# Attention's value products: the two heads of a pair in turn, key block by key block

## The chip, the cores and the metric

The kernel runs on one core of a Trainium2 chip. The time is device microseconds (us) of one execution on that core. Three runs of the kernel before took 1001.0, 1001.56 and 1004.53 us; the median is 1001.56.

## The reference, cut to what matters

```python
# q, k, v: [batch 4, heads 8, seq 576, head_dim 64]
scores = q @ k.transpose(0, 1, 3, 2) / sqrt(64)
rel = pos[:, None] - pos[None, :]
mask = (rel >= 0) & (rel < 128)                 # each query sees itself and 127 keys before it
scores = where(mask, scores - slopes[h] * abs(rel), -1e9)
attn = softmax(scores)
x = attn @ v                                    # -> [2304 tokens, 8 * 64 = 512]
x = (silu(x @ w_gate) * (x @ w_val)) @ w_out    # layer 1, hidden 1536
h = x @ w_in                                    # layer 2, hidden 2048
return (h * tanh(softplus(h))) @ w_out2
```

## The kernel before, in words

The 2304 tokens (four sequences of 576) are cut into five chunks of 512, 384, 512, 512 and 384 (`A_CHUNKS`). They are numbered 0 to 4 here. Three phases follow each other. The attention of chunk 0 runs alone (to about 59 us). Then layer 1 runs over the chunks (to about 637 us), and during layer 1 of chunk c the attention of chunk c+1 is mixed in. Layer 2 is last and has no attention in it.

Attention of a chunk works on query blocks of at most 128. For each head there are three kinds of work on TensorE, each as "pieces" that a planner places:

- S (`score`, lines 204 to 234): scores of one PSUM bank into `s_ps`. VectorE adds the bias and takes the row minimum (L226), ScalarE takes the exponential (L230); after the head's last bank come `norm` and the splitting of the next head's q and k.
- T (`transp`, L251): the normalised weights `Pt` are transposed by TensorE into `t_ps` (L259), and ScalarE copies them to `PT` (L271).
- O (`outp`, L274): the value products. The 64 value dimensions of head 0 of a pair go to partitions 0 to 63 of the bank `o_ps`, those of head 1 to partitions 64 to 127. Each key block contributes one product: its values `v` (up to 128 keys by 64) are the weights, and the columns of `PT` that belong to the queries seeing that block are streamed. ScalarE and VectorE then write the two halves of `xt` (a rounded part and the rest), and the values of the pair after next are loaded by DMA on SyncE's queue (`load_v`, L181).

The operands of O are plain fp32, and each product is executed as two passes, each with a weight load (LDWEIGHTS) and a MATMUL. There are four O pieces per chunk. For one head of one pair the key blocks (keys x streamed columns) are, in the order before:

- chunk 0: 128x256, 128x256, 128x256 and 128x128, in order of `par`;
- chunk 1: 64x64, 128x256, 64x64, 128x64, 128x192;
- chunk 2: 128 keys throughout, two of 256 columns and three of 128;
- chunk 3: 128x256, 64x64, 128x192, 128x128, 128x192, 64x64;
- chunk 4: 128 keys throughout, two of 256 columns and two of 128.

The sum of the columns over two heads and two passes is 3584, 2560, 3584, 3584 and 3072.

Layer 1 consists of groups of 12 products: two "g" groups (`g_ps`, `hid`) per hidden tile, and one "o" group (`acc`, `proj`). TensorE's instructions stand in the order in which the program emits them (`manual_schedule`, L912). The loop from L985 emits one group and then as many attention pieces as the planner's costs allow: pieces are spread so that the share of their cost that is spent keeps pace with the share of groups done (L998). S pieces have costs 1.7 or 0.87, T 0.44, and O the number of key blocks times 0.86 (`o_piece`, L356). The order on the other engines is worked out by a scheduler from this program. The banks of `g_ps`, `s_ps`, `t_ps` and `o_ps` rotate through four buffers (`rot`).

Of the kernel before, what the change touches and what calls it, by code (L numbers as in the profile page):

```python
# [37 lines left out]
def chunk_plan(t0, n):  # L38

    segs, qb, kb = [], [], []  # L40
    done = 0
    koff = 0
    while done < n:
        b, s0 = divmod(t0 + done, S)
        m = min(n - done, S - s0)
        kn0 = min(W, s0)
        segs.append(SimpleNamespace(b=b, s0=s0, n=m, c0=done, kn0=kn0, koff=koff))
        first = len(qb)
        prevkb = None
        if kn0:  # L50
            prevkb = SimpleNamespace(b=b, k0=s0 - kn0, n=kn0, uses=[], par=1, seg=len(segs) - 1)
            kb.append(prevkb)
        o = 0
        while o < m:
            qn = min(W, m - o)
            q0 = s0 + o
            kn = min(W, q0)
            q = SimpleNamespace(qn=qn, kn=kn, c=done + o, ko=koff + kn0 + o - kn, idx=len(qb))
            own = SimpleNamespace(b=b, k0=q0, n=qn, uses=[], par=(len(qb) - first) % 2, seg=len(segs) - 1)
            if prevkb is not None:  # L60
                prevkb.uses.append((q, 0))
            own.uses.append((q, 1))
            qb.append(q)
            kb.append(own)
            prevkb = own
            o += qn
        done += m
        koff += kn0 + m
    for i, x in enumerate(kb):
        x.vi = i  # L70
        x.w = sum(q.qn for q, _ in x.uses)
        assert all(q.kn == x.n for q, o in x.uses if o == 0)
        assert all(x.uses[i + 1][0].c == x.uses[i][0].c + x.uses[i][0].qn for i in range(len(x.uses) - 1))
    nbanks = -(-sum(q.kn + q.qn for q in qb) // 512)
    sb = [[[], 0] for _ in range(nbanks)]
    for q in sorted(qb, key=lambda q: -(q.kn + q.qn)):
        x = next(x for x in sb if x[1] + q.kn + q.qn <= 512)
        q.so = x[1]
        x[0].append(q)
        x[1] += q.kn + q.qn  # L80
    order = sorted(kb, key=lambda x: (x.n != 128))
    full = [x for x in order if x.n == 128]
    part = [x for x in order if x.n != 128]
    nbanks = -(-sum(x.w for x in kb) // 512)
    tb = [[[], 0] for _ in range(nbanks)]
    for x in sorted(full, key=lambda x: -x.w) + part:
        i = next(i for i in range(nbanks) if tb[i][1] + x.w <= 512)
        x.bank = i
        x.bo = tb[i][1]
        tb[i][0].append(x)  # L90
        tb[i][1] += x.w
    o_order = sorted(kb, key=lambda x: x.par)
    return SimpleNamespace(t0=t0, n=n, segs=segs, qb=qb, kb=kb, sb=sb, tb=tb, o_order=o_order, nk=koff)


# [1 line left out]
def body(ctx: ExitStack, tc: tile.TileContext, qT, kT, vP, w1, w1o, w2, cst, yT):  # L97
# [18 lines left out]
    def mm(out, lhsT, rhs, start, stop):  # L116
        nc.tensor.matmul(out=out, lhsT=lhsT, rhs=rhs, start=start, stop=stop, skip_group_check=True)  # L117

    def rot(name):
        return ps.tile([128, 512], F32, tag="rot", name=name)  # L120


    def hi_act(out, in_):
        return nc.scalar.activation(out=out, in_=in_, func=AF.Copy)  # L124

    def lo_dve(out, in_, hi):
        return nc.vector.tensor_tensor(out=out, in0=in_, in1=hi.bitcast(F32), op=ALU.subtract)  # L127
# [3 lines left out]
    for n in A_CHUNKS:  # L131
        plansA.append(chunk_plan(t, n))
        t += n
# [4 lines left out]
    def attention(ap, p, ci, s_native, upfront):  # L138


        raw, qk, pt_, P_, sums = {}, {}, {}, {}, {}
# [132 lines left out]
        def outp(pr):  # L274
            v = raw.pop(("v", pr))
            xt = x_t[ci]
            n = p.n
            o_ps = rot("o_ps")
            for e in range(2):
                st = True  # L280
                for x in p.o_order:
                    c0 = x.uses[0][0].c
                    mm(
                        o_ps[64 * e:64 * e + 64, c0:c0 + x.w], v[:x.n, x.vi, 64 * e:64 * e + 64],
                        pt_[2 * pr + e, x.bank][:x.n, x.bo:x.bo + x.w], st, False,
                    )
                    st = False
            hi_act(xt[:, 0, pr, :n], o_ps[:, :n])
            lo_dve(xt[:, 1, pr, :n], o_ps[:, :n], xt[:, 0, pr, :n])

        return SimpleNamespace(
            ci=ci, load=load, load_v=load_v, split=split, score=score, norm=norm, transp=transp,
            outp=outp, upfront=upfront, ns=len(p.sb), nt=len(p.tb), s_full=s_full, nk=len(p.kb),
        )

    early = {}

    def attention_pieces(atts):

        heads = [(a, h) for a in atts for h in range(H)]  # L300
        pairs = [(a, r) for a in atts for r in range(HP)]
        n = len(heads)
        out = []

        def run(k, f):
            a, h = heads[k]
            return getattr(a, f)(h)

        def load(k):
            if not heads[k][0].upfront:  # L310
                run(k, "load")

        def load_v(r):
            if not pairs[r][0].upfront:
                pairs[r][0].load_v(pairs[r][1])

        def first():
            if atts[0].upfront:
                for h in range(0, H, 2):
                    run(h, "load")  # L320
                    for f in early.pop(h, []):
                        f()
            load(0)
            load_v(0)
            run(0, "split")
            load(1)
            load_v(1)

        def s_piece(k, g):
            a, h = heads[k]  # L330

            def f():
                if k == 0 and g == 0:
                    first()
                a.score(h, g)
                if g == a.ns - 1:
                    a.norm(h)
                    if k + 1 < n:
                        run(k + 1, "split")
                        if k + 2 < n:  # L340
                            load(k + 2)

            return (a.ci, 1.7 if a.s_full(h) else 0.87, f)

        def o_piece(k):
            a, h = heads[k]

            def f():
                if a.ci not in x_t:
                    x_t[a.ci] = xp.tile([128, 2, CT, 512], F32R, tag="x", name="xt")  # L350
                a.outp(h // 2)
                r = a.ci * HP + h // 2 + 2
                if r < len(pairs):
                    load_v(r)

            return (a.ci, a.nk * 0.86, f)  # L356

        def t_piece(k, g):
            a, h = heads[k]
            return (a.ci, 0.44, lambda: a.transp(h, g))  # L360

        def delay(k):
            return CFG["delay0"] if heads[k][0].ci == 0 else 1

        for st in range(n + 4):
            todo = {"S": [], "T": [], "O": []}
            if st < n:
                todo["S"] = [s_piece(st, g) for g in range(heads[st][0].ns)]
            for k in range(max(0, st - 4), min(st, n)):
                if k + delay(k) == st:  # L370
                    todo["T"] += [t_piece(k, g) for g in range(heads[k][0].nt)]
                if k + delay(k) + 1 == st and heads[k][1] % 2 == 1:
                    todo["O"].append(o_piece(k))
            for c in CFG["order"]:
                if todo[c]:
                    out.append(todo[c].pop(0))
            for c in "SOT":
                out += todo[c]
        out.sort(key=lambda x: x[0] > 0)
        return out  # L380
# [531 lines left out]
    with tc.manual_schedule(engines={mybir.EngineType.PE}):  # L912
# [26 lines left out]
        while at < lasts[0]:  # L939
# [11 lines left out]
            f = (at / lasts[0] - CFG["conv_a"]) / (CFG["conv_b"] - CFG["conv_a"])  # L951
# [3 lines left out]
        for ci, p in enumerate(plansA):  # L955
# [29 lines left out]
            for gi, (kind, i, f) in enumerate(groups):  # L985
# [12 lines left out]
                while win and (spent * ng < (gi + 1) * total or gi == len(groups) - 1):  # L998
                    _, cost, e = win.popleft()
# [78 lines left out]
```

## Time and profile before

| what | value |
|---|---|
| runs | 1001.0, 1001.56, 1004.53 us |
| profiled execution, from first to last instruction (span) | 1002.2 us |
| TensorE (PE) busy | 966.8 us, 96% |
| VectorE (DVE) busy | 706.7 us, 71% |
| ScalarE (ACT) busy | 555.0 us, 55% |
| GpSimd (POOL) busy | 137.4 us, 14% |
| chain that ended last | PE 29% of the span, DVE 2%, DMA 1% |

The span is all that the profile tells of its execution's time. It lies 0.6 us above the median of the runs and inside their spread, so nothing outside the span has to be added. PE is the matmul side of TensorE and PEld its weight loads, which can overlap matmuls. A matmul's end is modelled in the profile: one that streams 256 columns is shown as some 0.38 us long while the next starts earlier. So times of matmuls are read here from start to start.

### The profile page before, as it was taken

The numbers are of one execution on the slowest core, as the hardware profiler recorded it, in microseconds if no ns is written. First come the engines' busy times: TensorE is split into PE (matmuls) and PEld (weight loads), VectorE is DVE, ScalarE is ACT, GpSimd is POOL, SyncE is SP. The second block draws the span as 40 slices with busy tenths as digits, with TensorE's granted clock in tenths as the row PEclk, the third lists the DMA queues.
The fourth block names the chain that finished last, engine by engine and source line by source line (L and its number), as shares of the span: only waits on it lengthen the run. The fifth ranks groups of instructions, "written<-read, shape, count | busy, mean of one in ns | idle before, by whom it ended". The sixth has DMA issues, their size and how long they took to land. (4 is left out here: it accounts for less than half of the span.)

```text
span 1002.2 us, 14578 instructions
## 1 busy us (share of the span) xinstructions
PE 966.8 (96%) x5168; PEld 854.4 (85%) x5168; DVE 706.7 (71%) x1263; ACT 555.0 (55%) x1135; POOL 137.4 (14%) x204
## 2 busy tenths in 40 slices
PE   6899999999999999999999999899999999999998
PEld 4557777898997877788787999789999999999998
DVE  4989898686586644647843576787795888867773
ACT  6857566666677555544643345555463555545342
POOL 2610000000000000000001233454002330022000
PEclk8989999999999999999999999999999999999999
DMA  8854433566454632326610898432787137850275
GB/s 303 283 208 146 136 120 114 183 214 199 129 166 152 215 110 69 101 65 227 233 43 22 298 374 293 169 116 84 243 260 254 64 109 269 291 172 22 82 248 195
DMA packets 76920, 174.82 MB, mean 174 GB/s; under 512 B 9136, under 2 KB 52528, under 8 KB 67120
## 3 DMA queue, kind: packets, MB, share of 16 engines
q1 hardware_dynamic: 76848, 173.90, 51.9%
q8 instruction: 40, 0.66, 0.3%
q14 instruction: 32, 0.26, 0.1%
HBM read 138.22 MB, written 35.65 MB: 173 GB/s over the span
## 5 line engine op out<-in xcount | busy, mean ns | idle before, releaser
L117 PE MATMUL g_ps<-xt,w 128*128 128x512 f32 (+1 forms) x1440 | 316.4, 372 | 1.1 <-ACT PT L271 1.1
L117 PEld LDWEIGHTS g_ps<-xt,w 128*128 128x128 f32 x1440 | 258.4, 188 | 38.0 <-ACT PT L271 2.2
L117 PE MATMUL bk<-xs,win 128*128 128x384 f32 x1008 | 179.1, 336 | 7.5 <-DVE G L679 5.4
L117 PEld LDWEIGHTS bk<-xs,win 128*128 128x128 f32 x1008 | 174.4, 188 | 11.8 <-DVE G L679 9.0
L117 PE MATMUL bk<-op,wout 128*128 128x384 f32 x1008 | 175.5, 334 | 0.5 <-DMA wout<-w2o 0.5
L117 PEld LDWEIGHTS bk<-op,wout 128*128 128x128 f32 x1008 | 174.8, 188 | 0.8 <-issue 0.8
L117 PE MATMUL acc<-hh,ring 128*128 128x512 f32 (+1 forms) x480 | 149.4, 374 | 1.6 <-DVE ring L127 1.6
L124 ACT ACTIVATE op<-G 128x768 fp32r<-128x768 f32 x84 | 70.8, 846 | 65.6 <-PE bk L117 63.1
L117 PEld LDWEIGHTS acc<-hh,ring 128*128 128x128 f32 x480 | 88.9, 188 | 15.4 <-DVE ring L127 2.3
L127 DVE TENSOR_TENSOR op<-G,op 128x768 fp32r<-128x768 f32 x84 | 80.5, 965 | 26.9 <-ACT op L124 26.3
L117 PE MATMUL acc<-hl,ring 128*128 128x512 f32 (+1 forms) x240 | 88.4, 368 | 0.0
L230 ACT ACTIVATE Pt<-Pt,sm 128x256 f32<-128x256 f32 (+2 forms) x160 | 74.3, 466 | 14.8 <-DVE sm L226 14.5
L613 ACT ACTIVATE t<-g_ps 128x512 f32<-128x512 f32 (+1 forms) x60 | 32.9, 549 | 78.8 <-PE g_ps L117 78.6
L614 DVE SCALAR_TENSOR_TENSOR t<-t,g_ps 128x512 f32<-128x512 f32 (+1 forms) x60 | 37.7, 629 | 53.0 <-ACT t L613 53.0
L226 DVE CUSTOM_DVE_ANT_0 Pt<-s_ps,cst_sb 128x256 f32<-128x256 f32 (+2 forms) x160 | 54.2, 376 | 27.7 <-PE s_ps L117 19.4
L775 POOL TENSOR_TENSOR t<-w 128x256 f32<-128x256 f32 x48 | 42.5, 905 | 224.1 <-DVE win L127 211.3
L622 DVE SCALAR_TENSOR_TENSOR t<-t,g_ps 128x512 f32<-128x512 f32 (+1 forms) x60 | 37.9, 632 | 37.0 <-PE g_ps L117 36.0
L1023 ACT ACTIVATE G<-G 128x384 f32<-128x384 f32 x72 | 36.8, 520 | 44.4 <-DVE G L679 44.4
L679 DVE TENSOR_TENSOR G<-u,bk 128x384 f32<-128x384 f32 x72 | 39.0, 552 | 31.3 <-PE bk L117 29.2
L124 ACT ACTIVATE hh<-t 128x512 fp32r<-128x512 f32 (+1 forms) x60 | 34.9, 582 | 43.8 <-DVE t L622 43.8
L259 PE MATMUL t_ps<-cst_sb,Pt 128*128 128x128 f32 (+2 forms) x288 | 47.0, 279 | 7.7 <-POOL Pt L249 4.2
L247 ACT ACTIVATE Pt<-Pt,sm 128x256 f32<-128x256 f32 (+2 forms) x128 | 50.1, 465 | 7.1 <-DVE sm L241 7.0
(75 smaller groups left out, 1250.8 us busy)
## 6 DMA issues: line engine op xcount, KB each, us to landing
wout<-w2o SPq DMA_DIRECT2D x42, 1024.0 KB, 6.4
wraw<-w SPq DMA_DIRECT2D x16, 1024.0 KB, 5.7
w2o<-chl SPq DMA_DIRECT2D x16, 896.0 KB, 8.7
wst<-w SPq DMA_DIRECT2D x12, 1024.0 KB, 7.4
cw<-w1od SPq DMA_DIRECT2D x24, 512.0 KB, 3.9
w<-w2d SPq DMA_DIRECT2D x24, 512.0 KB, 3.3
w2d<-cw SPq DMA_DIRECT2D x16, 512.0 KB, 4.6
wraw<-w1o SPq DMA_DIRECT2D x6, 1024.0 KB, 6.1
```

The source lines that it names most:

```text
L117: nc.tensor.matmul(out=out, lhsT=lhsT, rhs=rhs, start=start, stop=stop, skip_group_check=True)
L124: return nc.scalar.activation(out=out, in_=in_, func=AF.Copy)
L127: return nc.vector.tensor_tensor(out=out, in0=in_, in1=hi.bitcast(F32), op=ALU.subtract)
L226: nc.vector.tensor_tensor_reduce(out=Pt[:q.qn, :w], in0=s_ps[:q.qn, q.so:q.so + w], in1=nb[:q.qn, 128 - q.kn:128 + q.qn], op0=ALU.add, op1 ...
L230: nc.scalar.activation(out=Pt[:q.qn, :w], in_=Pt[:q.qn, :w], func=AF.Exp, scale=-1.0, bias=sm[:q.qn, i:i + 1], accum_out=sm[:q.qn, 8 + i:9 ...
L247: nc.scalar.activation(out=pt, in_=pt, func=AF.Copy, scale=r)
L259: nc.tensor.transpose(t_ps[:x.n, o:o + q.qn], Pt[:q.qn, c0:c0 + x.n], ident[:q.qn, :q.qn])
L614: nc.vector.scalar_tensor_tensor(out=t[:, :n], in0=t[:, :n], scalar=1.0, in1=st["g"][:, :n], op0=ALU.add, op1=ALU.mult)
L622: nc.vector.scalar_tensor_tensor(out=t[:, :n], in0=t[:, :n], scalar=0.5, in1=vps[:, :n], op0=ALU.mult, op1=ALU.mult)
L679: nc.vector.tensor_tensor(out=out, in0=a, in1=b, op=op)
L775: nc.gpsimd.tensor_tensor(out=x[:, o], in0=a, in1=b, op=ALU.subtract)
L1023: nc.scalar.activation(out=out, in_=in_, func=AF.Mish)
```

## The change

The loops of `outp` change places: for each key block, first the product of head 0 and then the product of head 1. The blocks with 128 keys now come first and the shorter ones last (`o_order`). The cost of an O piece in the planner falls from 0.86 to 0.46 per key block, which moves pieces between the groups.

```diff
-    o_order = sorted(kb, key=lambda x: x.par)
+    o_order = sorted(kb, key=lambda x: (x.n != 128, x.par))
...
-            for e in range(2):
-                st = True
-                for x in p.o_order:
-                    c0 = x.uses[0][0].c
+            for i, x in enumerate(p.o_order):
+                c0 = x.uses[0][0].c
+                for e in range(2):
                     mm(
                         o_ps[64 * e:64 * e + 64, c0:c0 + x.w], v[:x.n, x.vi, 64 * e:64 * e + 64],
-                        pt_[2 * pr + e, x.bank][:x.n, x.bo:x.bo + x.w], st, False,
+                        pt_[2 * pr + e, x.bank][:x.n, x.bo:x.bo + x.w], i == 0, False,
                     )
-                    st = False
...
-            return (a.ci, a.nk * 0.86, f)
+            return (a.ci, a.nk * 0.46, f)
```

On TensorE, the first O piece of chunk 1 stands in the order before as follows. `PT_761` and `PT_737` are the two banks of head 0, `PT_877` and `PT_867` those of head 1; 64x256 is 64 value dimensions by 256 columns.

```order
L117 MATMUL o_ps_991<-PT_761,v_492 64x64
L117 MATMUL o_ps_991<-PT_737,v_492 64x256
L117 MATMUL o_ps_991<-PT_761,v_492 64x64
L117 MATMUL o_ps_991<-PT_737,v_492 64x64
L117 MATMUL o_ps_991<-PT_737,v_492 64x192
L117 MATMUL o_ps_991<-PT_877,v_492 64x64
L117 MATMUL o_ps_991<-PT_867,v_492 64x256
L117 MATMUL o_ps_991<-PT_877,v_492 64x64
L117 MATMUL o_ps_991<-PT_867,v_492 64x64
L117 MATMUL o_ps_991<-PT_867,v_492 64x192
```

The same piece on TensorE in the changed kernel, where `PT_756` and `PT_784` are the banks of head 0, `PT_898` and `PT_926` those of head 1:

```order
L117 MATMUL o_ps_1029<-PT_756,v_492 64x256
L117 MATMUL o_ps_1029<-PT_898,v_492 64x256
L117 MATMUL o_ps_1029<-PT_756,v_492 64x64
L117 MATMUL o_ps_1029<-PT_898,v_492 64x64
L117 MATMUL o_ps_1029<-PT_756,v_492 64x192
L117 MATMUL o_ps_1029<-PT_898,v_492 64x192
L117 MATMUL o_ps_1029<-PT_784,v_492 64x64
L117 MATMUL o_ps_1029<-PT_926,v_492 64x64
L117 MATMUL o_ps_1029<-PT_784,v_492 64x64
L117 MATMUL o_ps_1029<-PT_926,v_492 64x64
```

The products are the same ten; the heads alternate, and the four products with 64 keys (banks `PT_784` and `PT_926`) have moved to the end.

The second place on TensorE is the last O piece of chunk 1, near the end of layer 1 of chunk 0. Before:

```order
L117 MATMUL s_ps<-KL,Q 128x128
L117 MATMUL o_ps<-PT,v 64x64
L117 MATMUL o_ps<-PT,v 64x256
L117 MATMUL o_ps<-PT,v 64x64 x2
L117 MATMUL o_ps<-PT,v 64x192
L117 MATMUL o_ps<-PT,v 64x64
L117 MATMUL o_ps<-PT,v 64x256
L117 MATMUL o_ps<-PT,v 64x64 x2
L117 MATMUL o_ps<-PT,v 64x192
L117 MATMUL g_ps<-xt,w 128x512 x24
L117 MATMUL acc_712<-hh,ring 128x512
```

And in the changed kernel:

```order
L117 MATMUL s_ps<-KL,Q 128x128
L117 MATMUL g_ps<-xt,w 128x512 x12
L117 MATMUL o_ps<-PT,v 64x256 x2
L117 MATMUL o_ps<-PT,v 64x64 x2
L117 MATMUL o_ps<-PT,v 64x192 x2
L117 MATMUL o_ps<-PT,v 64x64 x4
L117 MATMUL acc_693<-hh,ring 128x512
```

In both, the first `g_ps` group of chunk 1 (128x384), which reads what this piece yields, stands behind the 12 `acc` products. The piece has moved from three groups ahead of it to one group ahead, and it now follows a `g_ps` group where it followed an S piece.

## Rows read from the trace of the kernel before

**Rows 1.** Stages: us, busy us per engine (instructions), granted clock, DMA share, GB/s.

```profile
0.00:59.00 59.00, 43.63 (x185) 29.46 (x186) 42.94 (x118) 41.65 (x103) 27.22 (x52) 0.86 0.88 308
59.00:190.00 131.00, 128.37 (x617) 95.23 (x618) 116.95 (x237) 87.77 (x202) 1.39 (x9) 1.00 0.42 139
190.00:560.00 370.00, 365.78 (x1927) 306.73 (x1926) 221.21 (x483) 208.48 (x502) 8.41 (x23) 1.00 0.43 138
560.00:1002.00 442.00, 429.06 (x2443) 423.01 (x2441) 325.57 (x428) 217.10 (x331) 100.42 (x120) 1.00 0.58 198
```

**Rows 2.** Groups by shape, O pieces, chunks 1 to 4: busy, mean ns | idle before.

```profile
L117 PE MATMUL o_ps<-PT,v 128*64 128x256 f32 x96 | 27.1, 396 | 1.6 <-DVE sm L226 1.6
...
L117 PE MATMUL o_ps<-PT,v 64*64 64x64 f32 x64 | 10.4, 243 | 0.0
```

**Rows 3.** Timeline of PE, one O piece of chunks 2, 3, 4: start, length, instruction.

```profile
209.05 2.87 PE L117 MATMUL o_ps<-PT,v 128*64 128x256 f32 x20
211.85 0.44 PE L117 MATMUL acc<-hh,ring 128*128 128x384 f32 x1
...
318.45 4.27 PE L117 MATMUL o_ps<-PT,v 128*64 128x256 f32 x24
322.65 0.50 PE L117 MATMUL acc<-hh,ring 128*128 128x512 f32 x1
...
459.05 2.22 PE L117 MATMUL o_ps<-PT,v 128*64 128x256 f32 x16
461.20 0.51 PE L117 MATMUL g_ps<-xt,w 128*128 128x512 f32 x1
```

**Rows 4.** Timeline of weight loads, one O piece of chunk 1 and what follows.

```profile
102.89 0.45 PEld L117 LDWEIGHTS o_ps<-PT,v 64*64 64x64 f32 x4 [0.36 <-DVE sm L241]
103.72 0.56 PEld L117 LDWEIGHTS o_ps<-PT,v 64*64 64x64 f32 x6 [0.39 <-issue]
104.56 0.45 PEld L117 LDWEIGHTS o_ps<-PT,v 64*64 64x64 f32 x4 [0.28 <-issue]
105.39 0.56 PEld L117 LDWEIGHTS o_ps<-PT,v 64*64 64x64 f32 x6 [0.38 <-issue]
106.24 0.30 PEld L117 LDWEIGHTS g_ps<-xt,w 128*128 128x128 f32 x2 [0.28 <-issue]
```

**Rows 5.** Timeline of PE at four moments (35.15, 35.36, 35.63, 35.86): products in flight.

```profile
34.96 0.38 PE L117 MATMUL o_ps<-PT,qkv 128*64 128x256 f32 x1
...
35.17 0.38 PE L117 MATMUL o_ps<-PT,qkv 128*64 128x256 f32 x1
...
35.39 0.59 PE L117 MATMUL o_ps<-PT,qkv 128*64 128x256 f32 x3
...
35.61 0.49 PE L117 MATMUL o_ps<-PT,qkv 128*64 128x256 f32 x3
```

**Rows 6.** The stretch with the lower clock at the end of chunk 0's attention.

```profile
51.80:58.60 6.80, 5.81 (x19) 3.24 (x20) 5.11 (x7) 2.67 (x4) 1.73 (x2) 0.50 1.01 426
```

**Rows 7.** Timeline of weight loads, last O piece of chunk 0 and what follows.

```profile
54.10 0.29 PEld L117 LDWEIGHTS o_ps<-PT,qkv 128*64 128x64 f32 x2 [0.33 <-ACT w L124]
...
55.01 0.23 PEld L117 LDWEIGHTS o_ps<-PT,qkv 128*64 128x64 f32 x1 [0.20 <-issue]
55.44 0.23 PEld L117 LDWEIGHTS o_ps<-PT,qkv 128*64 128x64 f32 x1 [0.20 <-issue]
...
58.85 0.30 PEld L117 LDWEIGHTS g_ps<-xt,w 128*128 128x128 f32 x2 [0.17 <-issue]
```

**Rows 8.** Timeline of PE behind the third O piece of chunk 0.

```profile
47.57 0.33 PE L259 MATMUL t_ps<-cst_sb,Pt 128*128 128x128 f32 x1 [1.02 <-POOL Pt L249]
```

**Rows 9.** Timeline of PE and of DVE behind the last O piece of chunk 1.

```profile
186.01 4.17 PE L117 MATMUL g_ps<-xt,w 128*128 128x512 f32 x17
...
188.13 0.56 DVE L127 TENSOR_TENSOR xt<-o_ps,xt 128x384 fp32r<-128x384 f32 x1
```

**Rows 10.** DMA issues: count, KB each, median us to landing.

```profile
v<-vP SPq DMA_DIRECT2D x64, 64.0 KB, 2.3
```

## The prediction

> **What bounds the kernel now.** I read the stages first. From 59 to 190 us, where layer 1 of chunk 0 carries the attention of chunk 1, TensorE is busy 128.37 of 131 us; from 190 to 560 us, with the attention of chunks 2 to 4, 365.78 of 370 us [rows 1]. So in these 501 us TensorE idles only 2.6 + 4.2 = 6.8 us. VectorE is the next engine: 117 of 131 us in the first of the two stretches, 221 of 370 in the second. TensorE's own time is what sets the end there, and a microsecond taken from it is a microsecond of the kernel, unless VectorE then comes late. Before 59 us it is different: TensorE is busy 43.6 of 59 us and waits for the softmax on other engines; for instance it idles 1.02 us for GpSimd's scaling behind the third O piece [rows 8]. Behind 560 us nothing of the change is executed.
>
> Next I asked what an O piece costs, from the start of its first product to the start of what follows. In chunk 1 it is 106.24 - 102.89 = 3.35 us [rows 4]; in chunk 2 211.85 - 209.05 = 2.80, in chunk 3 322.65 - 318.45 = 4.20, in chunk 4 461.20 - 459.05 = 2.15 us [rows 3]. With four pieces per chunk that is 4 x 12.50 = 50.0 us of TensorE.
>
> Last, how an O piece passes its time. Successive passes of 256 columns start at 34.96, 35.17, 35.39 and 35.61 us [rows 5]: 0.65 / 3 = 0.217 us each, 0.846 ns per column. The columns of a piece then give, one after the other, 2560 x 0.846 = 2.17 us in chunk 1, 3584 x 0.846 = 3.03 in chunks 2 and 3, 3072 x 0.846 = 2.60 in chunk 4. Two things separate these from the measured times:
>
> - Chunks 1 and 3 take longer by 1.18 and 1.17 us. Both have pieces in which products with 64 keys stand between products with 128, in eight runs of one kind each (four per head). The weight loads of chunk 1 show the breaks: where one kind follows the other they pause 0.28 to 0.39 us [rows 4]. That is 1.18 / 8 = 0.148 and 1.17 / 8 = 0.146 us per run; I take 0.147.
> - Chunks 2 and 4 have one run each, so they should take 3.18 and 2.75 us, and take less by 0.38 and 0.60. The reason is in [rows 5]: at 35.36 us one product is in flight, at 35.63 three. Two of these started at 35.39, one for each head; the third at 35.61. So a product of head 1 streams while head 0 streams, and neither is slower for it: the starts stay 0.22 us apart. Before, this happens only where the end of head 0 meets the start of head 1.
>
> **The change part by part.** *Alternation.* Each product of one head now has one of the other head right behind it, with the same number of columns, for other partitions of the same bank. That is the situation of [rows 5] throughout, so the streaming time should halve. *The new order of blocks.* Every piece with short blocks has two runs instead of eight. The piece then costs half the columns plus 0.147 us per run:
>
> - chunk 1: 1.085 + 2 x 0.147 = 1.38 us, saved 1.97;
> - chunk 2: 1.515 + 0.147 = 1.66 us, saved 1.14;
> - chunk 3: 1.515 + 0.294 = 1.81 us, saved 2.39;
> - chunk 4: 1.30 + 0.147 = 1.45 us, saved 0.70.
>
> Together 6.20 us, times four pieces 24.8 us.
>
> One thing is not in the trace of before: two products with 64 keys, one for each head, side by side. Their head-to-head transition always meets a run of the other kind. If they pair as the others do, the above holds. If they only follow each other, the four passes of 64 columns that pairing would have hidden cost 4 x 64 x 0.846 = 0.22 us per piece in chunks 1 and 3, 8 x 0.22 = 1.7 us in all. If every change of head among them breaks like a change of kind, three more runs come on top, 8 x (0.22 + 0.44) = 5.3 us. From below, they cannot be better than paired. I take paired, since the nearest rows, products with 128 keys in the same two column halves, pair [rows 5], and keep 5.3 us for the range.
>
> The Trainium skill, "TensorE: Matmul & The Clock Gate", section "Packing small matmuls — row/col tiling", says that matmuls start and end in strict program order. By that rule a piece would still overlap, but the heads would run one pass apart, and each of the 16 pieces would end a pass later: an estimate of 16 x 0.217 = 3.5 us less saved, 21.3. The trace disagrees: at 35.39 us the first pass of head 1 has started while passes of head 0 that stand ahead of it in the program (that of 35.61 among them) have not. I keep the full pairing.
>
> *Chunk 0.* Its last piece takes from 54.10 to 58.85 us [rows 7], at a granted clock of 0.50 [rows 6], that is 1.2 GHz: passes of 256 columns are 55.44 - 55.01 = 0.43 us apart. Paired it would take 1792 x 0.43 / 256 + 2 x 0.147 = 3.3 us, 1.45 less. But the clock rises at 58.6, and until then the work that moves up runs at half speed, so half of it counts: 0.7 us. Behind it stand `g_ps` products on which nothing else is late. The other three pieces shorten too, but the time behind them belongs to GpSimd, ScalarE and VectorE [rows 8], so I count nothing there. Bounds: 0 to 2 us for all four.
>
> *What moves with the pieces.* The last O piece of chunk 1 comes two groups later. Behind it stand only the 12 `acc` products and the first nine products of the next group, a little over 4 us, before `xt` of this pair is read (17 products of 512 columns take 4.17 us with a modelled end [rows 9]; 12 of them and nine of 384 columns make 12 x 0.245 + 9 x 0.245 x 3/4 = 4.6 us by that, somewhat less in truth). Before, VectorE had written it 188.13 + 0.56 - 186.01 = 2.7 us after the piece [rows 9], behind three longer instructions in its queue. A cover of 4 us holds; if VectorE were 2 us later still, up to 0.7 us would be lost at this one place. The piece's load of values by SyncE moves with it; it lands 2.3 us after issue [rows 10] and is needed two pieces later, tens of microseconds on, so it costs nothing. The wait that O pieces had for VectorE's reduction (1.6 us, when a piece stood right behind an S piece and wanted its bank buffer) [rows 2] should go in chunk 2, where a `g_ps` group now stands between at all four places. Other waits of this kind will come, because VectorE has less time per group: I leave the 6.8 us of idle time as it is, with -2 and +4 as bounds.
>
> **Sum.** 24.8 + 0.7 = 25.5 us. The span of the profiled execution is 1002.2 us, 0.6 above the median of the runs, so the term applies to the median: 1001.56 - 25.5 = 976.
>
> **The rivals.**
>
> 1. *VectorE takes the place of TensorE.* From 59 to 190 us it is busy 89% [rows 1]. With 7.9 us less the stretch would be 123 us, VectorE at 95%, and its idle time is itself made of waits. If the stretch keeps its length, the 4 x 1.97 of chunk 1 are lost: 976 + 7.9 = 984 us. Against it: TensorE idles only 2.6 us there now, so VectorE is on time nearly always, and its conversion of weights can slip into the stretch behind, where it is busy 60%.
> 2. *The heads do not pair when they alternate strictly.* If the overlap needs several products of one head in a row, only the runs are saved: 2.17 + 0.29, 3.18, 3.03 + 0.29 and 2.75 make 11.71 per set against 12.50, 4 x 0.79 = 3.2 us, so 998.4 us. For it: all overlap seen is between a tail and a head. Against it: in [rows 5] the two streams go on side by side over several starts.
> 3. *The two streams slow each other,* by a quarter: the paired streaming time of 5.42 us per set becomes 6.77, 4 x 1.35 = 5.4 us, so 981 us. Against it: starts 0.22 us apart, alone or paired [rows 5]. The page named above gives 2.38 times for three column groups, 0.79 of the ideal; by that factor my sum would lose an estimated 5.6 us.
> 4. *Slower: each change of head breaks the flow* as a change between 64 and 128 keys does, at 0.147 us. Products per piece are 10, 10, 12 and 8, each now a run of its own: 3.64, 4.50, 4.79 and 3.78 us, 16.71 per set against 12.50, 4 x 4.21 = 16.8 us more, 1018 us. It decides from 0.11 us per change on. For it: the column half is changed at every product, which before happened once per piece. Against it: the one such change per piece before shows overlap, not a break, in chunks 0, 2 and 4.
>
> **How the numbers follow.** Forecast 0.71, rival 1 in whole or part 0.14, rival 2 0.06, rival 3 0.05, rival 4 0.04. Faster by over 0.5% (below 996.5; about what a measurement of this kernel can tell from no change): 0.71 + 0.14 + 0.05 = 0.90. Within 0.5%: 0.06. Slower: 0.04. The forecast's own range is 976 - 4 (waits go, chunk 0 gains 2) to 976 + 9 (5.3 for the short blocks, 4 for waits), less its corners: 972 to 984. With half of rival 1 beyond 984, and rival 3, the range is 971 to 986.
>
> **What would show it.** In the profile after: O pieces of 1.4, 1.7, 1.8 and 1.45 us from first start to the next instruction; weight loads in pairs, with one pause per piece in chunks 1 and 3; TensorE still busy over 97% from 59 us on, and layer 2 starting some 25 us earlier with its length unchanged. Pieces of 2.4 to 3.3 us would mean rival 2, of 3.6 to 4.8 rival 4; pieces as short as forecast, with new idle time on TensorE released by VectorE in the first stretch, rival 1. The forecast is wrong if pieces do not fall to about half, or if the layer 1 stretches give the time back as idle time.

## The result, and the profile after

The changed kernel took 986.54 us (median of 983.84, 985.22, 987.85 and 992.29) against 1001.28 us for the kernel before: ratio 0.9845, 95% interval 0.9812 to 0.9878. In a second comparison on one chip it took 983.31 us (979.45 to 987.22) against 1002.77: ratio 0.9813, interval 0.9785 to 0.9841. Between 15 and 19 us are gained, where the forecast was 25.5. The first median lies 0.5 us above the stated range of 971 to 986, the second inside it. The profiled execution of the changed kernel has a span of 986.1 us, the second one ("again" below) 981.5 us.

First the O pieces. These are the weight loads of the first O piece of chunk 1 in the changed kernel, which answer to [rows 4], and what follows:

```profile
110.43 0.74 PEld L117 LDWEIGHTS o_ps<-PT,v 128*64 128x64 f32 x12 [0.35 <-issue]
111.46 0.31 PEld L117 LDWEIGHTS o_ps<-PT,v 64*64 64x64 f32 x8 [0.28 <-issue]
111.83 0.53 PEld L117 LDWEIGHTS g_ps<-xt,w 128*128 128x128 f32 x3
```

Four groups of loads with a pause before each have become two: 12 loads for blocks of 128 keys, one pause, 8 loads for blocks of 64. The piece takes 111.83 - 110.43 = 1.40 us; it took 3.35. The timeline of TensorE for pieces of chunks 2, 3 and 4, which answers to [rows 3]:

```profile
207.39 1.74 PE L117 MATMUL o_ps<-PT,v 128*64 128x256 f32 x20
209.06 0.45 PE L117 MATMUL g_ps<-xt,w 128*128 128x384 f32 x1
...
313.99 1.90 PE L117 MATMUL o_ps<-PT,v 128*64 128x256 f32 x24
315.82 0.50 PE L117 MATMUL g_ps<-xt,w 128*128 128x512 f32 x1
...
445.38 1.52 PE L117 MATMUL o_ps<-PT,v 128*64 128x256 f32 x16
446.83 0.50 PE L117 MATMUL acc<-hh,ring 128*128 128x512 f32 x1
```

From start to start 1.67, 1.83 and 1.45 us, where it was 2.80, 4.20 and 2.15. All sixteen pieces of chunks 1 to 4 agree with these within 0.01 us. So 4 x (1.95 + 1.13 + 2.37 + 0.70) = 24.6 us of TensorE are gone, as forecast. Then the stages, cut where layer 1 of the next chunk and layer 2 begin (columns as in [rows 1]):

```profile
0.00:60.02 60.02, 43.40 (x184) 30.87 (x184) 42.46 (x117) 42.09 (x102) 27.98 (x52) 0.77 0.87 314
60.02:188.64 128.62, 126.25 (x637) 95.41 (x637) 116.09 (x238) 88.02 (x206) 1.73 (x9) 1.00 0.40 127
188.64:292.49 103.85, 99.73 (x637) 94.71 (x636) 75.75 (x177) 71.15 (x176) 0.83 (x8) 0.98 0.60 191
292.49:536.91 244.42, 243.53 (x1253) 194.60 (x1253) 143.99 (x304) 133.25 (x321) 4.56 (x11) 1.00 0.40 128
536.91:616.97 80.06, 78.24 (x446) 77.24 (x444) 56.08 (x71) 40.20 (x58) 28.26 (x33) 1.00 0.88 307
616.97:986.07 369.10, 355.57 (x2017) 350.53 (x2016) 268.55 (x359) 178.14 (x275) 75.02 (x92) 1.00 0.52 174
```

Set beside the same cuts in the other profiles (us):

| stage | before | forecast of the difference | after | again |
|---|---|---|---|---|
| attention of chunk 0 | 58.86 | -0.7 | 60.02 | 58.12 |
| layer 1, chunk 0 (with pieces of chunk 1) | 135.48 | -7.9 | 128.62 | 130.27 |
| layer 1, chunk 1 (pieces of chunk 2) | 105.39 | -4.6 | 103.85 | 101.80 |
| layer 1, chunks 2 and 3 (pieces of 3 and 4) | 257.10 | -12.4 | 244.42 | 244.69 |
| layer 1, chunk 4 (no pieces) | 80.03 | 0 | 80.05 | 81.58 |
| layer 2 | 365.38 | 0 | 369.10 | 365.08 |

Where TensorE is bound and nothing else is near (chunks 2 and 3) the stage gives back what the pieces saved: 12.7 and 12.4 us. What is missing lies in the other stages, and not in the same ones both times: 9.3 us in the first profile (1.9 in chunk 0's attention, 1.0 and 3.0 in the layer 1 stages of chunks 0 and 1, 3.7 in layer 2, 0.3 won in chunks 2 and 3), 4.8 us in the second. One thing that differs is TensorE's clock. These are stretches of the first profile of the changed kernel:

```profile
222.00:226.66 4.66, 3.00 (x18) 2.48 (x18) 4.66 (x14) 3.62 (x8) 0.00 (x0) 1.00 0.58 213
226.66:230.07 3.41, 3.41 (x12) 3.23 (x12) 3.35 (x6) 3.30 (x9) 0.00 (x0) 0.50 0.93 359
...
634.00:646.50 12.50, 8.41 (x47) 7.77 (x46) 10.58 (x14) 5.83 (x11) 6.22 (x6) 1.00 0.36 135
646.50:649.91 3.41, 3.41 (x12) 3.41 (x12) 1.34 (x3) 2.21 (x4) 1.52 (x3) 0.50 0.00 0
```

Before each fall TensorE was busy for only 3.00 of 4.66 and 8.41 of 12.5 us; then 3.41 us pass at the granted clock 0.50 (1.2 instead of 2.4 GHz), though TensorE is busy throughout. What that costs can be read from two groups of twelve like products, one at the full clock and one that begins 0.46 us before the first fall:

```profile
205.17 2.29 PE L117 MATMUL g_ps<-xt,w 128*128 128x384 f32 x12
...
226.20 3.86 PE L117 MATMUL g_ps<-xt,w 128*128 128x384 f32 x12 [0.81 <-DVE sm L226]
```

The difference is 1.57 us, so a stretch costs some 1.6 us. The first profile has two behind 60 us, the second three (from 150.8, 611.6 and 635.5 us): 3.2 and 4.7 us. The kernel before has none there in its first profile.

### The profile page after: what moved, and what is told of

The parts are those of the page before. It is cut to its first block, busy times and chain, and to the rows that moved or that the text cites. A ratio compares the mean times of both kernels' runs of the same rounds, so it can differ in the third digit from the quotient of the medians.

```text
span 986.1 us, 14581 instructions
## 1 busy us (share of the span) xinstructions
PE 946.7 (96%) x5168; PEld 843.4 (86%) x5168; DVE 702.9 (71%) x1263; ACT 552.9 (56%) x1135; POOL 138.4 (14%) x204
## 4 chain that ended last, share of the span: by engine, by line
PE 76%; DVE 8%; DMA 7%; ACT 3%; issue 2%; POOL 2%; SPq 1%; DVEq 0%; POOLq 0%; ACTq 0%
PE bk L117 31%; PE g_ps L117 25%; PE acc L117 12%; DMA wraw<-w 4%; PE s_ps L117 3%; PE o_ps L117 3%; PE t_ps L259 3%; POOL Pt L249 1%; POOL t L773 1%; DMA w<-w2d 1%; DVE G L677 1%; DVE Pt L226 1%; DVE cw L433 1%; DMA wout<-w2o 1%; SPq L181 1%
## 5 line engine op out<-in xcount | busy, mean ns | idle before, releaser
L117 PE MATMUL g_ps<-xt,w 128*128 128x512 f32 (+1 forms) x1440 | 320.6, 375 | 1.7 <-ACT PT L271 0.9
L230 ACT ACTIVATE Pt<-Pt,sm 128x256 f32<-128x256 f32 (+2 forms) x160 | 74.3, 466 | 15.6 <-DVE sm L226 15.3
L226 DVE CUSTOM_DVE_ANT_0 Pt<-s_ps,cst_sb 128x256 f32<-128x256 f32 (+2 forms) x160 | 54.4, 376 | 27.3 <-PE s_ps L117 27.0
L259 PE MATMUL t_ps<-cst_sb,Pt 128*128 128x128 f32 (+2 forms) x288 | 49.9, 288 | 10.0 <-POOL Pt L249 8.9
L259 PEld LDWEIGHTS t_ps<-cst_sb,Pt 128*128 128x128 f32 (+2 forms) x288 | 34.9, 144 | 27.3 <-POOL Pt L249 12.7
```

The lines of the kernel that those rows point to most:

```text
L226: nc.vector.tensor_tensor_reduce(out=Pt[:q.qn, :w], in0=s_ps[:q.qn, q.so:q.so + w], in1=nb[:q.qn, 128 - q.kn:128 + q.qn], op0=ALU.add, op1 ...
L230: nc.scalar.activation(out=Pt[:q.qn, :w], in_=Pt[:q.qn, :w], func=AF.Exp, scale=-1.0, bias=sm[:q.qn, i:i + 1], accum_out=sm[:q.qn, 8 + i:9 ...
L259: nc.tensor.transpose(t_ps[:x.n, o:o + q.qn], Pt[:q.qn, c0:c0 + x.n], ident[:q.qn, :q.qn])
```

## The experiments

"Waits" are TensorE's, of over 0.3 us beyond the streaming time of a product (0.423 ns per column, in O pieces 0.846), from start to start, in the layer 1 stages of chunk 0 and of chunk 1. "Clock" counts stretches at 0.50 behind 61 us and before the last 25 us.

| run | O pieces, chunks 1 to 4 (us) | waits (us) | clock | median us | ratio to before (interval) |
|---|---|---|---|---|---|
| before | 3.34, 2.80, 4.20, 2.15 | 3.2, 3.5 | 0 | 1001.28 | |
| b_again | the same | 3.2, 2.8 | 1 | 1003.6 (one run) | |
| after | 1.40, 1.67, 1.83, 1.45 | 2.8, 4.9 | 2 | 986.54 | 0.9845 (0.9812 to 0.9878) |
| a_again | the same | 2.8, 4.4 | 3 | 983.31 | 0.9813 (0.9785 to 0.9841) |
| e1_cost86 | as after | 3.6, 3.5 | 2 | 983.51 | 0.9814 (0.9793 to 0.9835) |
| e2_cost46_only | as before | 1.4, 0 | 0 | 1000.24 | 0.9977 (0.9960 to 0.9994) |
| e3_alt_oldblocks | 1.70, 1.67, 2.13, 1.45 | 2.8, 3.8 | 2 | 983.55 (one run) | |
| e4_blocks_only | 2.78, 2.80, 3.63, 2.15 | 1.4, 1.0 | 0 | 997.05 (one run) | |
| e5_by_two | 2.11, 1.72, 1.89, 1.50 | 3.2, 6.2 | 4 | 995.33 (one run) | |
| e7_chunk0_serial | as after | 1.4, 2.0 | 0 | 981.79 | 0.9803 (0.9775 to 0.9831) |
| e8a_prefetch | as after | 2.9, 2.9 | 2 | 980.56 | 0.9787 (0.9762 to 0.9811) |
| e8b_delay | as after (one of 2.07, with a wait inside) | 2.8, 4.5 | 1 | 982.51 | 0.9815 (0.9790 to 0.9840) |
| e9_hl_gpsimd | as after | 0, 4.6 | 3 | 982.23 | 0.9796 (0.9778 to 0.9815) |
| e10_both | as after | 2.6, 5.6 | 4 | 985.04 | 0.9815 (0.9794 to 0.9835) |

**How the pieces come to their times.** Two kernels each do one half of the change to the products; their edits are shown against the changed kernel. e3_alt_oldblocks alternates and keeps the old order of blocks:

```diff
-    o_order = sorted(kb, key=lambda x: (x.n != 128, x.par))
+    o_order = sorted(kb, key=lambda x: x.par)
```

> Alternation of the heads, but the key blocks in the old order, so that products with 64 keys again stand between products with 128. Forecast's theory (half the columns, plus 0.147 us for each run of one kind): four runs instead of two in chunks 1 and 3, O pieces of 1.67 and 2.10 us there, 1.67 and 1.45 in chunks 2 and 4. Rival F (a change of kind costs nothing once heads alternate): 1.40, 1.67, 1.83 and 1.45 as in the changed kernel.

The pieces of chunks 1 and 3 took 1.70 and 2.13 us; expected 1.67 and 2.10. The timeline of TensorE shows two of chunk 1 and what follows them:

```profile
107.85 1.77 PE L117 MATMUL o_ps<-PT,v 64*64 64x64 f32 x20
109.55 5.78 PE L117 MATMUL g_ps<-xt,w 128*128 128x512 f32 x24
...
159.05 1.77 PE L117 MATMUL o_ps<-PT,v 64*64 64x64 f32 x20
160.75 3.04 PE L117 MATMUL g_ps<-xt,w 128*128 128x512 f32 x12
```

e4_blocks_only has the new order of blocks and the new planner cost, but the loop over heads outside:

```diff
-            for i, x in enumerate(p.o_order):
-                c0 = x.uses[0][0].c
-                for e in range(2):
+            for e in range(2):
+                st = True
+                for x in p.o_order:
+                    c0 = x.uses[0][0].c
```

> The new block order and the new planner cost, but head after head as before. Forecast's theory (full columns, 0.147 us per run, four runs per piece in chunks 1 and 3): O pieces of 2.76, 2.80, 3.62 and 2.15 us. Rival G (the saving in chunks 1 and 3 is the alternation's alone): 3.34, 2.80, 4.20 and 2.15 us.

2.78, 2.80, 3.63 and 2.15 us: within 0.02 of the sum by columns and runs. So both halves count: of 6.1 us saved per set of four pieces, grouping the blocks alone gives 1.1 and alternation alone 5.5 (together less than their sum, since alternation halves the number of breaks by itself).

e5_by_two lets the heads take turns every two blocks (the changed kernel's two loops become one over this list):

```diff
+            steps_.sort(key=lambda s: (s[0] // 2, s[2]))
+            for i, x, e in steps_:
```

> The changed kernel, but the heads take turns every two key blocks (four passes of one head, then four of the other). Forecast's theory (a product of the other column half starts as soon as it comes within three passes of the one that streams, as seen before at the join of the heads): pairing holds, the second head runs about one pass late, and O pieces take 0.1 to 0.3 us more than in the changed kernel: about 1.6, 1.8, 2.05 and 1.6 us. Rival K (pairing needs the partner right behind): the first and last two blocks run alone, and pieces take 0.9 us more or worse, 2.3 us and up.

In chunks 2 to 4 the pieces are 0.05 us longer than in the changed kernel: four passes of one head in a row do not stop the other from streaming beside them. In chunk 1 the piece is 2.11 us, where 1.6 was expected; there the groups of two mix blocks of 128 and of 64 keys. That adds two breaks between kinds (0.29 us), and the blocks of 192 columns stand on either side of a break: their products start at 111.30 us for one head and at 111.98 us for the other, so these do not run side by side. The rival falls. The whole kernel, 995.33 us in its one run, is slower by far more than its pieces (4 x 0.87 = 3.5 us): its waits are 9.4 us in these two stages and four stretches fall to the lower clock.

**Is the missing part at fixed places?** The changed kernel once more:

> The changed kernel once more, to get a second profile and a narrower interval. All theories: 986.5 us, O pieces of 1.40, 1.67, 1.83 and 1.45 us in chunks 1 to 4. Theory A (the 9 us that the forecast has too much are lost at fixed places: the attention of chunk 0 about 2, the layer 1 stage of chunk 1 about 3, the start of layer 2 about 4, and the order of instructions sets them): the same waits at the same places again, within 0.5 us each. Rival B (they are chance: the clock falls in some executions): the waits and the stretches at the lower clock stand elsewhere, and the time differs by 3 us or more from the first profile's.

Neither as theory A nor quite as its rival. The waits near 150, 223 to 226 and 635 us came back within 0.2 us of their sizes, but those that end at 255, 281 and 646 us (1.4, 1.5 and 2.1 us) did not, and the clock fell at other places. The kernel before, once more:

> The kernel before, once more, for a second profile. Behind 59 us its first profile has the full clock throughout, though TensorE waits for about 8 us in layer 1; the changed kernel's two profiles have two and three stretches of 3.4 us at the lower clock there, each right behind such waits. Theory D (waits of TensorE that stand close together bring the clock down in some executions, in either kernel): one or two such stretches may stand in this profile too. Rival E (only the changed kernel has them): none behind 59 us again. O pieces of 3.34, 2.80, 4.20 and 2.15 us, 1000 to 1004 us in both.

One fall, at 662 us:

```profile
655.00:662.40 7.40, 5.11 (x30) 4.79 (x29) 7.19 (x10) 2.85 (x5) 3.51 (x4) 1.00 0.21 71
662.40:665.80 3.40, 3.40 (x13) 3.40 (x12) 1.95 (x3) 2.16 (x4) 3.32 (x4) 0.50 0.00 0
```

TensorE is busy 5.11 of the 7.40 us before it. So the kernel before has such falls too, rival E is out, and theory D holds as far as it goes: falls stand behind waits, in either kernel and not in each execution. Over all profiles there are 23 falls in the ten of kernels that alternate and one in the four of kernels that do not, each of them behind a wait; e7_chunk0_serial, which alternates in chunks 1 to 4, has none. That they are more frequent with alternation is a count, not a cause that was tested.

**The planner's cost.** e1_cost86 is the changed kernel with the old cost, e2_cost46_only the kernel before with the new one:

```diff
-            return (a.ci, a.nk * 0.46, f)
+            return (a.ci, a.nk * 0.86, f)
```

```diff
-            return (a.ci, a.nk * 0.86, f)
+            return (a.ci, a.nk * 0.46, f)
```

> Alternation and new block order, but the planner's cost of an O piece as before (0.86): the pieces stand between the groups as in the kernel before. Theory A: O pieces save 24.6 us as in the changed kernel, the waits in the layer 1 stages of chunks 0 and 1 are those of the kernel before (about 6.6 us instead of 7.7 and a fall of the clock), chunk 0's attention and the start of layer 2 stay as in the changed kernel: 982 to 984 us. Rival C (VectorE comes late because TensorE is faster, wherever the pieces stand): the waits stay or grow, 986 us or more.

> The planner's cost alone (0.46); the products stay head by head in the old block order. O pieces take 3.34, 2.80, 4.20 and 2.15 us as before. Theory A: the new places of the pieces cost 1 to 3 us of waits in the layer 1 stages of chunks 0 and 1: 1002 to 1004 us. Rival C: the places cost nothing by themselves, 1001 us.

Neither theory holds in both runs. In e2_cost46_only the new places of the pieces cost nothing by themselves: they gain 0.2% (interval 0.06 to 0.4%), and the waits go down to 1.4 us, against theory A. In e1_cost86 the waits, 3.6 and 3.5 us, are near those of the kernel before, and 983.51 us is what theory A expected and 2.5 us below rival C's least. So shorter pieces bring waits with the new cost (1.4 us in e2_cost46_only, 7.7 and 7.2 in the changed kernel) and next to none with the old one (6.6 before, 7.0 in e1_cost86). That the pieces are shorter does not explain the waits alone; where they stand, and the order that the other engines get with it, counts too, and which wait comes from which stays open. The time does not show which cost is used with alternation (983.51 and 983.31 us).

The new places have a price that the table does not show. The gaps of under 0.3 us between products, summed over the layer 1 stages of chunks 0 to 3, are 56.9 us in the kernel before and 57.2 in e1_cost86, with the old places, but 58.1 in e2_cost46_only and 58.3 and 58.7 in the changed kernel.

**Who is waited for.** In the second profile of the changed kernel, VectorE in the stage of chunk 1, followed by TensorE in the same microseconds:

```profile
219.03 0.55 DVE L612 SCALAR_TENSOR_TENSOR t<-t,g_ps 128x384 f32<-128x384 f32 x1
221.67 0.69 DVE L428 TENSOR_SCALAR cw<-wraw 128x1024 int32<-128x1024 int32 x1 [2.09 <-DMA wraw<-w]
222.28 0.55 DVE L620 SCALAR_TENSOR_TENSOR t<-t,g_ps 128x384 f32<-128x384 f32 x1
222.74 1.22 DVE L433 SCALAR_TENSOR_TENSOR cw<-wraw,cw 128x1024 f32<-128x1024 uint32 x1
223.88 0.42 DVE L226 CUSTOM_DVE_ANT_0 Pt<-s_ps,cst_sb 128x256 f32<-128x256 f32 x1
```

```profile
218.41 0.28 PE L117 MATMUL s_ps<-KL,Q 128*128 128x256 f32 x1
...
223.15 0.60 PE L259 MATMUL t_ps<-cst_sb,Pt 128*128 128x128 f32 x4
224.70 0.55 PE L259 MATMUL t_ps<-cst_sb,Pt 128*128 128x128 f32 x3 [0.95 <-DVE sm L226]
226.06 2.35 PE L117 MATMUL g_ps<-xt,w 128*128 128x384 f32 x12 [0.81 <-DVE sm L226]
```

The scores are written at about 218.5 us. VectorE reduces them at 223.88, because in its queue a conversion of layer 2 weights (L428) stands before, and waits 2.09 us for its load. In e2_cost46_only the same conversion waits 1.65 us until 223.96, but the scores come only at about 224.4, and the reduction follows some 2 us behind them, in time. So in the changed kernel the scores come 5.9 us earlier and the load 2.3 us earlier. The wait near 150 us is another: there TensorE waits 2.3 us for the splitting of q (L198). Two kernels try to take the wait for the load away. e8b_delay puts four empty steps ahead of the conversion:

```diff
-        steps(("w2d", i), [f0] + [lambda k=k: raw["f"][k]() for k in range(5)] + [f6])
+        steps(("w2d", i), [f0] + [lambda: None] * 4 + [lambda k=k: raw["f"][k]() for k in range(5)] + [f6])
```

> The changed kernel with four empty steps in the background list between the issue of the load of raw layer 2 weights (wraw) and its conversion, so that the conversion comes to VectorE later. In the second profile of the changed kernel VectorE stands still for 6.0 us between 59 and 230 us with a conversion at the head of its queue whose load has not landed (0.7 us in the kernel before), and the softmax reductions behind it make TensorE wait near 223 and 228 us. Theory H (this is what takes back part of the gain in the layer 1 stage of chunk 1): that wait falls under 2 us, TensorE's waits in this stage from 4.4 to under 2.5 us, the stage from 101.8 to about 99.5 us, the whole to 979 to 982 us. Rival C (VectorE is late because TensorE is faster, whatever stands in its queue): the waits stay, 983 to 986 us.

VectorE's waits by releaser from 59 to 300 us, first in the second profile of the changed kernel, then in e8b_delay (total us, times, longest):

```profile
DVE cw L428 <- DMA wraw<-w: 6.0, 2, 3.9
...
DVE ring L127 <- ACT ring L124: 3.5, 4, 1.5
```

```profile
DVE ring L127 <- ACT ring L124: 10.0, 7, 3.7
...
DVE cw L428 <- DMA wraw<-w: 2.3, 2, 1.5
```

The wait for `wraw` went down to 2.3 us, nearly as expected, and another took its place: at 221.63 us a ring half that waits 3.7 us for ScalarE stands at the head of VectorE's queue, and TensorE waits 4.5 us in this stage as before. Theory H falls. e8a_prefetch gives the load a second buffer, taken from that of `cg` (two become one), and issues it one conversion ahead:

```diff
-        stage[key] = bpool["a"].tile([128, 2048], I32, tag="wraw", name="wraw", bufs=1)
+        stage[key] = bpool["a"].tile([128, 2048], I32, tag="wraw", name="wraw", bufs=2)
...
-            stage_other(("2", i), w2[i])
+            for k in (i, i + 1):
+                if k < NF2 and k not in ahead:
+                    ahead.add(k)
+                    stage_other(("2", k), w2[k])
```

> The changed kernel with two buffers for the raw layer 2 weights (wraw), each load issued one conversion ahead; the buffer of the conversion's first step (cg) is cut from two to one to make room. In the changed kernel's second profile, and in those of e8b_delay and e9_hl_gpsimd, VectorE stands between 215 and 223 us with an instruction at the head of its queue whose data are not there (a conversion waiting for its load, or a ring half waiting for ScalarE), while finished scores wait behind it. Theory H2 (a load that is not paced by TensorE now lands late for a VectorE that runs in order): VectorE's wait for wraw between 59 and 300 us falls from 6.0 to under 1 us, TensorE's waits in the layer 1 stage of chunk 1 from 4.4 to under 2 us, the whole to 979 to 981 us. Rival M (as soon as one such instruction is gone another stands there, since VectorE's order is set with other times than the chip's): VectorE's wait for wraw goes, TensorE's waits stay above 3.5 us, 982 to 985 us.

```profile
DVE ring L127 <- ACT ring L124: 3.5, 4, 1.4
DVE cw L428 <- DMA wraw<-w: 1.1, 1, 1.1
```

VectorE's wait for `wraw` is 1.1 us, TensorE's waits in the stage 2.9 instead of 4.4: those near 223 us are gone, one of 2.2 us at 276 stays. That lies between H2 and rival M. The time, 980.56 us, is the lowest median of all, but its interval overlaps that of the changed kernel, and two falls of the clock stand in its profile.

e9_hl_gpsimd takes 60 instructions off VectorE:

```diff
-            lo_dve(hl[:, :n], t[:, :n], hh[:, :n])
+            nc.gpsimd.tensor_tensor(out=hl[:, :n], in0=t[:, :n], in1=hh[:, :n].bitcast(F32), op=ALU.subtract)
```

> The changed kernel with the rest of each hidden tile of layer 1 (hl = t - hh, 60 instructions of some 0.67 us on VectorE) computed by GpSimd, which is idle in layer 1. Theory C (VectorE is late because TensorE is faster; its load is what makes TensorE wait in the layer 1 stages of chunks 0 and 1): TensorE's waits there fall from 7.2 to under 4 us, and the time by 3 to 6 us, to 977 to 980 us. Rival L (the waits come from what stands in which order, not from the load): no gain, 983 us or more, or a loss where GpSimd's longer instruction (about 1.8 us) makes the acc products wait.

The waits in chunk 0's stage, 2.8 us, are gone; in chunk 1's they stay (4.6). That does not show that the load was the cause. In chunk 0's stage VectorE is busy 115.7 of 126.0 us here, where it was 116.9 of 130.3 in the second profile of the changed kernel, although 12 instructions are gone: some that run beside GpSimd's take longer. These are GpSimd and VectorE here, and the same kind of VectorE instruction in the second profile of the changed kernel:

```profile
211.14 1.91 POOL L630 TENSOR_TENSOR hl<-t,hh 128x384 fp32r<-128x384 f32 x1 [4.91 <-ACT hh L124]
212.09 1.24 DVE L418 TENSOR_SCALAR cp<-cg 128x512 int32<-128x512 int32 x1
```

```profile
224.56 0.42 DVE L418 TENSOR_SCALAR cp<-cg 128x512 int32<-128x512 int32 x1
```

VectorE's order changes with the edit too, and e7_chunk0_serial below has fewer waits in both stages (1.4 and 2.0 us) with nothing taken off VectorE. So theory C is not shown, and the 977 to 980 us that it expected did not come: 982.23 us is the time of the changed kernel within the intervals.

**Chunk 0 as before, and both together.** e7_chunk0_serial sorts the products of chunk 0 by head:

```diff
+            steps_ = [(i, x, e) for i, x in enumerate(p.o_order) for e in range(2)]
+            if ci == 0:
+                steps_.sort(key=lambda s: s[2])
+            for i, x, e in steps_:
```

> The changed kernel, but chunk 0's O pieces run head by head as before; chunks 1 to 4 alternate. VectorE's and ScalarE's order at the start of layer 2 is then that of the kernel before. Theory A: layer 1 begins at 58.9 us as before instead of 60.0, and the first 45 us of layer 2 lose 4 us instead of 8: 981 to 983 us. Rival B: as the changed kernel, 986 us.

The time is as theory A expected, but the waits in the first 45 us of layer 2 are 7.1 us, against 8.0 in the first profile of the changed kernel, 4.8 in the second and 6.3 in the kernel before: the loss that A put there did not come from this order. Layer 1 begins at 59.1 us. In the other kernels that alternate in chunk 0 it begins anywhere between 57.4 and 60.7 us, with two or three stretches at the lower clock in this part, in those that do not between 57.1 and 59.1, so alternation there neither gains nor loses anything that these runs can tell. The median of 981.79 us is not clear of a_again's.

> As e9_hl_gpsimd, and chunk 0's O pieces head by head as in e7_chunk0_serial; a candidate for a version better than both kernels. Theory C: 975 to 979 us. Rival L: as e7_chunk0_serial, 982 us.

985.04 us: the two do not add up, with 2.6 and 5.6 us of waits and four falls of the clock. Rival L is nearer. No version tried is clear of the changed kernel.

**Layer 2.** The change touches nothing there, and yet its first 45 us differ. VectorE, first in the changed kernel, then in the kernel before at the corresponding place:

```profile
631.43 1.23 DVE L127 TENSOR_TENSOR win<-w,win 128x768 fp32r<-128x768 f32 x1 [0.86 <-ACT win L124]
632.59 0.54 DVE L677 TENSOR_TENSOR u<-u,bk 128x384 f32<-128x384 f32 x1
634.39 1.22 DVE L127 TENSOR_TENSOR win<-t,win 128x1024 fp32r<-128x1024 f32 x1 [1.26 <-ACT win L124]
635.54 0.55 DVE L677 TENSOR_TENSOR u<-u,bk 128x384 f32<-128x384 f32 x1
```

```profile
651.80 1.20 DVE L679 TENSOR_TENSOR u<-u,bk 128x384 f32<-128x384 f32 x2
653.10 0.55 DVE L679 TENSOR_TENSOR G<-u,bk 128x384 f32<-128x384 f32 x1
654.42 1.23 DVE L127 TENSOR_TENSOR win<-t,win 128x1024 fp32r<-128x1024 f32 x1 [0.76 <-ACT win L124]
```

Before, both `u` sums come first and the half `win<-t` waits behind them. Now `win<-t` stands between them, and the second `u` waits with it; TensorE, which needs what follows, waits 2.17 us until 636.79:

```profile
636.79 1.50 PE L117 MATMUL bk<-xs,win 128*128 128x384 f32 x7 [2.17 <-DVE G L677]
```

The scheduler that orders VectorE's work has put it differently, some 100 us behind the last O piece. This order does not explain the longer layer 2. The second profile has it too, with a wait of 2.18 us there, and layer 2 takes 365.1 us, as before; and the kernel before has a wait of 2.08 us for the same kind of instruction somewhat later:

```profile
663.35 0.98 PE L117 MATMUL bk<-xs,win 128*128 128x384 f32 x4 [2.08 <-DVE G L679]
```

What the first profile has more is 2.4 us of waits over the whole layer (12.3 against 10.0; 8.6 in the second) and a fall of the clock, 1.6 us.

## Why the prediction was right or wrong

- *The price of a piece* (half the columns plus 0.147 us per run) was right: 1.38, 1.66, 1.81 and 1.45 us forecast, 1.40, 1.67, 1.83 and 1.45 measured. e3_alt_oldblocks and e4_blocks_only confirm each term. The open case, two products with 64 keys side by side, went as taken: without pairing the pieces of chunk 1 would have been 1.60 us or more. Rivals 2 (2.4 to 3.3 us), 3 (a quarter more streaming) and 4 (3.6 to 4.8 us) are out by the same numbers. Two halves side by side here give the ideal, 0.846 ns per column each. The Trainium skill ("TensorE: Matmul & The Clock Gate", section "Packing small matmuls — row/col tiling") gives 2.38 times for three column groups; that factor, 0.79 of the ideal, does not carry over to two. One figure of rival 4 was wrong: its pieces (10.83 us of columns and 40 products) cost more than the 12.50 us of before from 0.04 us per change on, not from 0.11.
- *Chunk 0, 0.7 us:* not settled. It began layer 1 1.2 us later in one profile, 0.7 us earlier in the other. The reasoning on its last piece took the lower clock to stand where it stood, from 51.8 to 58.6 us. It stood elsewhere: before layer 1 TensorE has 17.1 us at the lower clock in the kernel before, 27.3 and 23.9 us in the two profiles of the changed kernel. That the other three pieces would bring nothing agrees with the first profile: TensorE's waits for GpSimd's scaling (L249) grew there from 4.2 to 8.9 us (5.7 in the second).
- *The idle time "as it is":* right as a sum. TensorE idles 2.4 + 4.1 + 0.9 = 7.4 us in the layer 1 stages of chunks 0 to 3 (second profile 2.4 + 3.4 + 0.9 = 6.7), against 6.8 forecast. The stages of chunks 0 to 3 still gave 21.1 and 21.2 us instead of 24.6. Of the 3.5 and 3.4 us, one fall of the clock accounts for 1.6 in each profile, and gaps of under 0.3 us between products for 1.5 and 1.9, most of which e2_cost46_only has too: they come with the new places of the pieces, which the forecast put at nothing.
- *"A microsecond taken from TensorE is a microsecond of the kernel, unless VectorE comes late"* is the step that failed. Its sum had no term for the clock, which was full behind 59 us in the trace it read: two and three stretches of 3.41 us at half the clock take some 3.2 of the 9.3 us that are missing in the first profile, and nearly all of the 4.8 in the second. They stand behind waits, and waits of this size were there before; only those had not brought the clock down. That falls come more often with the changed kernel was not traced to a cause.
- *"Layer 2 with its length unchanged"* failed in one profile (369.1 us; 2.4 more waits and a fall of the clock) and held in the other (365.1).
- *Rival 1* is true in part, by another mechanism than its 95% load: one instruction that waits at the head of VectorE's in-order queue, for a load or for ScalarE, holds the reductions that TensorE needs. That is shown near 223 us, in chunk 1's stage. In chunk 0's stage, where the rival put up to 7.9 us, 1.0 and 2.7 us are missing, and TensorE's waits there are not longer than before (2.8 against 3.2 us).
- *The late `xt`* at the end of chunk 0's stage was covered, as worked out: no wait stands there.

## What to carry to other kernels

Products that use half of TensorE's columns should take turns between the halves, and products of one row count should stand together; what that gives can be read before the change from the one place where the halves already meet. Then subtract something: here the time taken from the bounding engine came back in full only in the stage of chunks 2 and 3, where VectorE was busy 59% of the time. Before such a forecast, look which queue has an instruction at its head that waits for a load, and what the clock does behind each wait, in more than one profile.

## What was not expected of the hardware

- TensorE starts a product of the other column half while three passes that stand before it in the program have not started: at the place of [rows 5] the first of head 1 starts at 35.40 us, and passes of head 0 at 35.61, 35.82 and 35.93. Pairing holds with four passes of one half in a row (e5_by_two, 0.05 us more per piece). Two streams do not slow each other: in the first piece of chunk 2 of the changed kernel pairs of 256 columns start at 207.66, 207.87 and 208.09 us, as far apart as single ones before.
- A change between products with 128 and with 64 rows costs 0.147 us, with one head or two: by this price the pieces of e3_alt_oldblocks and e4_blocks_only come out within 0.03 us.
- The granted clock falls to half for 3.41 us in the middle of a busy layer, behind waits of TensorE (it was busy 3.00 of 4.66, 8.41 of 12.5 and 5.11 of 7.40 us before three of the falls), and not in each execution. Single executions of one kernel differ by up to 8 us (983.84 to 992.29).
- A VectorE instruction of 0.42 us took 1.24 us beside one of GpSimd (e9_hl_gpsimd, 212.09 us), so work moved to GpSimd did not leave VectorE with less busy time.
